# The second layer's first product made of seven block products over pairs of 384 tokens, its weights split ahead of time and read back

## The chip, the cores and the metric

The kernel runs on one core of a Trainium2 chip. The metric is the device time of one execution in microseconds (us), taken as the median of the runs shown. Work is spread over TensorE (PE in the profile: matmuls, with its weight loads as PEld), VectorE (DVE), ScalarE (ACT), GpSimd (POOL) and the DMA queue that SyncE (SP) issues.

## The reference

Attention over 4 batches of 8 heads gives x of 2304 tokens by 512, and two feed-forward layers follow. All of it is in float32.

```python
xn = x / np.sqrt(np.mean(x * x, axis=-1, keepdims=True) + 1e-06) * rms_g
g, val = xn @ w_gate, xn @ w_val              # layer one, 512 to 1536
y = (g / (1 + np.exp(-g)) * val) @ w_out      # 1536 to 512
h = y @ w_in                                  # layer two, 512 to 2048: its first product
r = np.maximum(h, 0.0)
out = (r * r) @ w_out2                        # 2048 to 512: its second product
```

## The kernel before

Activations lie with features on the partitions and tokens along the row. **A float32 product is three matmuls.** Each operand is kept as a high part, rounded to the type that TensorE multiplies, and a low part, the rest; `mm3` (L1177 to L1182) adds high times high, high times low and low times high into one PSUM bank, so a product of 128 outputs with a contraction of 512 is 4 x 3 = 12 matmuls. The matmul lines L1180, L1181 and L1182 are these three, for every product of both layers.

The tokens go in five blocks (`BLOCKS`: four of 512 and one of 256). Each layer is cut into two phases over its hidden features (`PHASES`): layer one into two of 6 hidden tiles, layer two (phases 2 and 3) into two of 8 tiles of 128. In a phase all blocks run past the same weights, and for each block and hidden tile j, `ff_in` makes the hidden tile (in layer two 12 matmuls into a `gv` bank), `after_in` finishes it (layer two: ACT takes the relu out of PSUM at L1272, DVE multiplies it with the PSUM value at L1276, and the high part, L1283 or L1285, and the low part, L1290, are made), and `ff_out` (12 matmuls into the four `a` banks) adds it to the block's output one tile later. A block's first half of the sum goes out to `yp_d` and comes back for the second phase's eviction (L1384). Layer one's result goes to `y_d` and is read and split again for each of layer two's phases (`load_task`, `split_tasks`, L870 and L885).

**Weights** come packed in two words each. `w_task` loads two matrices (1 MB, `wst<-in_w`), puts the words together in five DVE or ACT steps of 1024 columns (L1106 or L1108, L1115, L1118, L1124, L1129) and splits them into high (L1138 or L1140) and low parts (L1146) in a ring of 13 places.

**Order.** A planner written in the kernel runs while the program is built. Every step is a task with a due number and a cost on an engine; `advance` takes the step that can start first, and among those within `TOL` of it the one with the lowest due number. What it settles is the fixed order of each engine's queue. PE's own order is written out by hand at the end (`steps`): `ff_in` of a tile, then `ff_out` of the tile before.

Of the kernel before, what the change touches and what calls it, by code (L numbers as in the profile page):

```python
# [49 lines left out]
NMAX = 512  # L50
# [42 lines left out]
PHASES = [(1, 0, 6, True, False), (1, 6, 6, False, True), (2, 0, 8, True, False), (2, 8, 8, False, True)]  # L93
# [90 lines left out]
def kernel(ctx: ExitStack, tc: tile.TileContext, loc, strd, w1, w2, g, cst, out):  # L184
    nc = tc.nc

    def pool(name, bufs, stack=ctx, **kw):
# [7 lines left out]
    wr_p = pool("wr", RING)  # L195
    wst_p = pool("wst", WST)
    x_p = pool("xhl", 2)
    hid_p = pool("hid", 2)
    tmp_p = pool("tmp", 2)
    ys_p = pool("ys", 1)  # L200
# [15 lines left out]
    norm0 = const.tile([128, BLOCKS[0][1]], F32)  # L216
# [7 lines left out]
    y1_d = [dram.tile([128, KDM, n], F32, name=f"y1_d{i}") for i, (_, n) in enumerate(BLOCKS)]  # L224
    yp_d = {
        ly: [dram.tile([128, KDM, n], F32, name=f"yp{ly}_d{i}") for i, (_, n) in enumerate(BLOCKS)]
        for ly in (1, 2)
    }
    src_d = [None, xn_d, y1_d, y1_d]
# [50 lines left out]
    def advance():  # L280
# [32 lines left out]
        near = [f for f in found[e] if -100 < f[1] < min(-40, due - 3) and f[0] < start + half]  # L313
# [539 lines left out]
    def split_tasks(key, due, n, src, before=None, after=None, got=None):  # L853
# [4 lines left out]
        def hi(k):  # L858
            def f(_, t):
                if "t" not in cell:  # L860
                    cell["t"] = x_p.tile([128, 2, KDM, NMAX], F32R, tag="x", name="xt")
                    take("x")
                    turn("x")
                    xhl_of[key] = cell["t"]
# [133 lines left out]
    def load_task(ph, i, due):  # L998
# [3 lines left out]
        def load(_, t):  # L1002
            take("xs")
            cell["t"] = late["xs"].tile([128, KDM, NMAX], F32, tag="xs", name="xs")
            nc.sync.dma_start(out=cell["t"][:, :, :n], in_=src_d[ph][i])
            turn("xs")
            spawn(
                split_tasks((ph, i), due, n, lambda k: [(0, cell["t"][:, k, :n])], after=lambda t: give("xs", t)),
                lanes.dma(KDM * n, t),
            )  # L1010

        tasks.append(Task(due, [(
            lambda: "xs" in late and room("xs") and in_turn("xs", nth_x[ph, i] - NB) and ("src", ph, i) in done,
# [5 lines left out]
    def yp_task(ph, i, due):  # L1019
        n = BLOCKS[i][1]  # L1020
        nth = (NB if PHASES[ph][0] == 2 else 0) + i

        def load(_, t):
            take("yp")
            v = late["yp"].tile([128, KDM, NMAX], F32, tag="yp", name="ypt")
            nc.sync.dma_start(out=v[:, :, :n], in_=yp_d[PHASES[ph][0]][i])
# [6 lines left out]
            lambda: "yp" in late and room("yp") and in_turn("yp", nth) and ("yp", ly, i) in done,  # L1033
# [4 lines left out]
    wst, wt, wst_from, raws = {}, {}, {}, []  # L1038
    wst_free = [[WST, wst_p]]
    rings = [[RING, deque(), wr_p]]  # L1040
    mats = [
        (ph, j, m) for ph, (ly, _, nj, _, _) in enumerate(PHASES) for j in range(nj) for m in range(3 if ly == 1 else 2)
    ]
    loaded = iter(range(len(mats) // 2))
# [8 lines left out]
    def put_w(n, landed):  # L1053
        ph, j, m = mats[2 * n]
        ly, f0 = PHASES[ph][:2]
        wd = w1 if ly == 1 else w2
        src = next(r for r in wst_free if r[0])
        src[0] -= 1
        wst_from[n] = src
        t = src[1].tile([128, 2, 512, 2], I32, tag="wst", name="wst")  # L1060
        o = (f0 + j) * wd.shape[1] + m
        nc.sync.dma_start(out=t, in_=wd.rearrange("j m p c w -> p (j m) c w")[:, o:o + 2])
        wst[n] = t
        done["wst", n] = landed

    def ring_free():
        return [r for r in rings if len(r[1]) < r[0] or r[1][0]["t"] is not None]

    def ring_time():
        rs = ring_free()  # L1070
        r = next((r for r in rs if len(r[1]) < r[0]), rs[0])
        return 0.0 if len(r[1]) < r[0] else r[1][0]["t"]

    def ring_take():
        rs = ring_free()
        r = next((r for r in rs if len(r[1]) < r[0]), rs[0])
        if len(r[1]) == r[0]:
            r[1].popleft()
        cell = {"t": None, "n": 0}
        r[1].append(cell)  # L1080
        return r[2].tile([128, 2, 2, 512], F32R, tag="w", name="w"), cell
# [6 lines left out]
    def w_task(n, due):  # L1088
        cell = {}
        keys = mats[2 * n:2 * n + 2]  # L1090

# [6 lines left out]
        def size(parts, t):  # L1098
            cell["w"], cell["ring"] = ring_take()
            if "raw" in late:  # L1100
                cell["r"] = late["raw"].tile([128, 2, 512], F32, tag="raw", name="raw")
# [26 lines left out]
        def bits2(_, t):  # L1128
# [4 lines left out]
            wst_from.pop(n)[0] += 1  # L1133
            load_w(t)
# [7 lines left out]
        def lo(e):  # L1142
            def f(parts, t):
# [7 lines left out]
        before = mats[2 * (n - NRAW) + 1] if n >= NRAW else None  # L1151
        tasks.append(Task(due, [
            (
                lambda: in_turn("bits", n) and n in wst and bool(ring_free()) and (before is None or before in wt)
                and (keys[0][0] == 0 or "raw" in late),
                [dvx(1024, fast=True), [("A", 1.14)]], size,
                lambda: max(
                done["wst", n], ring_time(), done["w", before] if before else 0.0, done["late"] if keys[0][0] else 0.0
            ),
            ),  # L1160
# [3 lines left out]
            (None, [dvx(1024)], bits2, None),  # L1164
            (None, [act(1024), dvx(1024, fast=True)], hi, None),
# [3 lines left out]


# [429 lines left out]
```

## Time and profile before

| | |
|---|---|
| median of 3 runs | 929.5 us (927.97 to 931.24) |
| span of the profiled execution | 926.5 us |
| PE busy | 913.9 us, 99% |
| DVE busy | 584.0 us, 63% |
| ACT busy | 284.6 us, 31% |
| POOL busy | 41.8 us, 5% |
| layer two on PE | from 525.92 us to about 922.3 us |

The span runs from the first to the last instruction of one execution; the time of a run also holds what lies around it. Busy time counts an instruction from its start to its end, and two matmuls in a row overlap, so that the distance from start to start is shorter than the duration shown. The rows from which the argument is made stand in a section of their own below.

### The profile page before, as it was taken

Reading aid. Unit: us, or ns where it says so; the run is one execution under the profiler, and the core shown is the slowest. Engines: PE = TensorE matmul, PEld = TensorE weight load, DVE = VectorE, ACT = ScalarE, POOL = GpSimd, SP = SyncE. Lnnn points to the kernel's source line nnn. Section 1 sums busy time; section 2 is a strip of 40 time slices with the busy share of each in tenths; the row PEclk is TensorE's granted clock in tenths of the full one; section 3 lists DMA queues with packets and bytes.
Section 4 is the critical chain, followed back from the end, with each engine's and each line's share of the span. In section 5 each row is a group of like instructions: output and inputs, shape, how many; then the busy total and the mean of one; then the engine's idle time right before and its main releaser. Section 6 shows DMA issues by size and latency. Waiting matters only on the chain.

```text
span 926.5 us, 15562 instructions
## 1 busy us (share of the span) xinstructions
PE 913.9 (99%) x6466; PEld 766.0 (83%) x6466; DVE 584.0 (63%) x960; ACT 284.6 (31%) x773; POOL 41.8 (5%) x37
## 2 busy tenths in 40 slices
PE   8999999999999999999999999999999999999998
PEld 4778778888889888888888988888889888888888
DVE  6999956536879999352436999643438835344443
ACT  5987764322234332010102424121214211111110
POOL 0334400000000000000000000000000000000000
PEclk9999999999999999999999999999999999999999
DMA  9866742411725444130201545320203203030201
GB/s 331 268 230 200 238 148 75 136 48 65 277 92 182 160 137 159 68 110 5 91 24 62 179 146 181 137 90 24 91 1 137 69 1 136 1 114 1 69 10 59
DMA packets 38150, 105.41 MB, mean 114 GB/s; under 512 B 4160, under 2 KB 17472, under 8 KB 33984
## 3 DMA queue, kind: packets, MB, share of 16 engines
q1 hardware_dynamic: 38080, 104.41, 33.2%
q8 instruction: 51, 0.84, 0.4%
q14 instruction: 19, 0.16, 0.1%
HBM read 77.20 MB, written 23.59 MB: 109 GB/s over the span
## 4 chain that ended last, share of the span: by engine, by line
PE 94%; DVE 2%; DMA 2%; ACT 1%; issue 0%; SPq 0%; DVEq 0%; ACTq 0%
PE gv L1180 18%; PE gv L1181 18%; PE gv L1182 17%; PE a L1180 12%; PE a L1181 12%; PE a L1182 12%; DMA wst<-in_w 2%; PE xo L526 1%; PE sc L390 1%; ACT sm L438 1%; PE bc L832 0%; DVE raws L1118 0%; PE ms L574 0%; PE msb L810 0%; PE a L481 0%; DVE hd L1290 0%
## 5 line engine op out<-in xcount | busy, mean ns | idle before, releaser
L1180 PE MATMUL gv<-xt,w 128*128 128x512 f32 (+1 forms) x800 | 296.7, 371 | 0.5 <-DVE t L1260 0.5
L1181 PE MATMUL gv<-xt,w 128*128 128x512 f32 (+1 forms) x800 | 294.6, 368 | 0.0
L1182 PE MATMUL gv<-xt,w 128*128 128x512 f32 (+1 forms) x800 | 294.4, 368 | 0.0
L1180 PE MATMUL a<-hd,w 128*128 128x512 f32 (+1 forms) x560 | 207.4, 370 | 0.0
L1181 PE MATMUL a<-hd,w 128*128 128x512 f32 (+1 forms) x560 | 206.2, 368 | 0.1
L1182 PE MATMUL a<-hd,w 128*128 128x512 f32 (+1 forms) x560 | 206.1, 368 | 0.0
L1180 PEld LDWEIGHTS gv<-xt,w 128*128 128x128 f32 x800 | 150.8, 189 | 26.1 <-DVE t L1260 0.6
L1182 PEld LDWEIGHTS gv<-xt,w 128*128 128x128 f32 x800 | 150.8, 189 | 25.2
L1181 PEld LDWEIGHTS gv<-xt,w 128*128 128x128 f32 x800 | 150.9, 189 | 24.6 <-DVE xt L880 0.3
L1276 DVE TENSOR_TENSOR t<-t,gv 128x512 f32<-128x512 f32 (+1 forms) x80 | 50.6, 633 | 165.0 <-ACT t L1272 165.0
L1272 ACT ACTIVATE t<-gv 128x512 f32<-128x512 f32 (+1 forms) x80 | 44.4, 555 | 296.8 <-PE gv L1182 296.8
L1180 PEld LDWEIGHTS a<-hd,w 128*128 128x128 f32 x560 | 105.6, 188 | 18.2 <-ACT pt L493 0.3
L1182 PEld LDWEIGHTS a<-hd,w 128*128 128x128 f32 x560 | 105.6, 188 | 17.6
L1181 PEld LDWEIGHTS a<-hd,w 128*128 128x128 f32 x560 | 105.6, 189 | 17.4 <-DVE hd L1290 0.3
L1290 DVE TENSOR_TENSOR hd<-t,hd 128x512 fp32r<-128x512 f32 (+1 forms) x138 | 89.2, 646 | 4.6
L1260 DVE SCALAR_TENSOR_TENSOR t<-t,gv 128x512 f32<-128x512 f32 (+1 forms) x60 | 37.9, 631 | 84.3 <-ACT t L1256 84.2
L1256 ACT ACTIVATE t<-gv 128x512 f32<-128x512 f32 (+1 forms) x48 | 26.1, 545 | 191.4 <-PE gv L1182 191.2
L1268 DVE TENSOR_TENSOR t<-t,gv 128x512 f32<-128x512 f32 (+1 forms) x60 | 37.9, 632 | 40.6 <-PE gv L1182 40.2
L1285 DVE CAST hd<-t 128x512 fp32r<-128x512 f32 (+1 forms) x133 | 53.1, 399 | 9.3
L885 DVE TENSOR_TENSOR xt<-xs,xt 128x512 fp32r<-128x512 f32 (+1 forms) x56 | 33.0, 648 | 0.2 <-ACT xt L870 0.2
L1146 DVE TENSOR_TENSOR w<-raw,w 128x512 fp32r<-128x512 f32 x48 | 31.6, 686 | 0.7 <-ACT w L1138 0.5
L1124 DVE SCALAR_TENSOR_TENSOR raw<-wst,raw 128x1024 int32<-128x1024 int32 x25 | 30.6, 1223 | 0.6
(96 smaller groups left out, 676.7 us busy)
## 6 DMA issues: line engine op xcount, KB each, us to landing
wst<-in_w SPq DMA_DIRECT2D x34, 1024.0 KB, 5.8
yp_d<-ys SPq DMA_DIRECT2D x8, 1024.0 KB, 4.7
ypt<-yp_d SPq DMA_DIRECT2D x8, 1024.0 KB, 7.0
xs<-y_d SPq DMA_DIRECT2D x8, 1024.0 KB, 5.1
qk<-in_strd SPq DMA_DIRECT2D x8, 604.0 KB, 6.3
qk<-in_loc SPq DMA_DIRECT2D x8, 592.0 KB, 4.7
xs<-xn_d SPq DMA_DIRECT2D x4, 1024.0 KB, 4.8
y_d<-ys SPq DMA_DIRECT2D x4, 1024.0 KB, 4.8
```

The source lines that it names most:

```text
L885: eng.tensor_tensor(out=cell["t"][:, 1, k, c], in0=x, in1=x_hi, op=ALU.subtract)
L1124: nc.vector.scalar_tensor_tensor(out=bits(), in0=word(1), scalar=-0x40000000, in1=bits(), op0=ALU.bitwise_and, op1=ALU.bitwise_or)
L1146: eng.tensor_tensor(out=w[:, 1], in0=cell["r"][:, e], in1=w[:, 0].bitcast(F32), op=ALU.subtract)
L1180: nc.tensor.matmul(out=o, lhsT=whi, rhs=x_hi, start=first, stop=False)
L1181: nc.tensor.matmul(out=o, lhsT=whi, rhs=x_lo, start=False, stop=False)
L1182: nc.tensor.matmul(out=o, lhsT=wlo, rhs=x_hi, start=False, stop=last)
L1260: nc.vector.scalar_tensor_tensor(out=t_sb[:, :n], in0=t_sb[:, :n], scalar=1.0, in1=ps[:, :n], op0=ALU.add, op1=ALU.mult)
L1268: nc.vector.tensor_tensor(out=t_sb[:, :n], in0=t_sb[:, :n], in1=ps[:, :n], op=ALU.mult)
L1272: nc.scalar.activation(out=tile_t()[:, :n], in_=ps[:, :n], func=ACTF.Relu)
L1276: nc.vector.tensor_tensor(out=t_sb[:, :n], in0=t_sb[:, :n], in1=ps[:, :n], op=ALU.mult)
L1285: nc.vector.tensor_copy(hid[key][0][:, 0, :n], tmps[key][:, :n])
L1290: eng.tensor_tensor(out=hd[:, 1, :n], in0=t_sb[:, :n], in1=hd[:, 0, :n].bitcast(F32), op=ALU.subtract)
```

## The change

Layer one keeps its phases and its order on PE. Layer two is rewritten. It still has two phases, each over half of the hidden features, but inside a phase the tokens go in three pairs (q) of 2 x 384, and the hidden features in four groups (j) of 2 x 128.

**The first product.** For a pair and a group the product is a 2 by 2 block product: two hidden tiles by two halves of the contraction (256 each), times two halves of the contraction by two token halves. Eight block products were needed; `PRODUCTS` lists seven (Winograd's form), on seven weight blocks (three plain, four sums) and seven token blocks (three plain, four differences). Each is 2 x 3 = 6 matmuls of 384 columns (L1791). P1, P6, P7 and P4 are added one after the other into one bank, A, and the bank's value is wanted in between. So a copy of A is taken after P1 (`s1`) before P6 may be added to it, another after P6 (`u2`) before P7, and the sum A + `s5` after P7 before P4; P5 has a bank D (copied as `s5`, then P3 is added) and P2 a bank C. The copies (L1812 on ACT or L1814 on DVE) and the sums (L1821, DVE) give the four hidden tiles; the fourth is a relu of A (L1832, ACT). Then come the square (L1844 and L1845 on ACT, L1847 on DVE), the high part (L1873 or L1875) and the low part (L1880).

**The second product** is as before, in matmuls of 384 columns. The first token half (n = 0) is added up between the products, one group later; the second half (n = 1) follows in eight steps at the end of the pair.

**The token blocks** are read from `y1_d` in four transfers a pair. Four differences (L1640), seven high parts (L1647 or L1649) and seven low parts (L1654) of 768 columns are made for each of the six pairs.

**The weights** of layer two are no longer used from where they are split. For each phase and group, `pieces` makes the four sums (L1278), splits all into high and low parts in two small stages (L1292 or L1294, L1315), stores them to DRAM (`wi_d`, `wo_d`, L1306), and `load2_task` reads them back (L1340), 1.75 MB for a group of `w_in` and 1 MB of `w_out`. The first phase's are made during layer one, the second's mostly during the first two pairs.

All pools become fixed places in four large tiles (`ra`, `rb`, `fa`, `fb`, with `wst_a`). The diff, cut to its core:

```diff
-PHASES = [(1, 0, 6, True, False), (1, 6, 6, False, True), (2, 0, 8, True, False), (2, 8, 8, False, True)]
+PHASES = [(1, 0, 6, True, False), (1, 6, 6, False, True)]
+SN, NQ, NJ = 384, NT // 768, 4
+PRODUCTS = [
+    ("P1", 0, 0, "A", None), ("P5", 3, 1, "D", None), ("P6", 4, 2, "A", "s1"), ("P2", 1, 3, "C", None),
+    ("P7", 5, 4, "A", "u2"), ("P3", 6, 5, "D", "s5"), ("P4", 2, 6, "A", "c22"),
+]
...
+            o, w, x = c[role]["ap"][:, :SN], w_in(j), x_slot2(b)
+            for k in range(2):
+                w_hi, w_lo = (w[:, e, 256 * a + 128 * k:256 * a + 128 * k + 128] for e in range(2))
+                for n, (l, r) in enumerate(((w_hi, x[:, 0, k]), (w_hi, x[:, 1, k]), (w_lo, x[:, 0, k]))):
+                    nc.tensor.matmul(
+                        out=o, lhsT=l, rhs=r, start=need is None and k + n == 0, stop=k == 1 and n == 2,
+                        skip_group_check=need is not None,
+                    )
...
+            "P1": lambda: copy("s1", "A"), "P5": lambda: copy("s5", "D"), "P6": lambda: copy("u2", "A"),
+            "P2": lambda: add("s1", "C", 0, 0), "P7": lambda: add("s5", "A", 1, 1), "P3": lambda: add("u2", "D", 0, 1),
+            "P4": lambda: relu(1, 0),
...
+            steps = [
+                total(1024, 512, 768, ALU.add), total(1280, 1024, 0, ALU.subtract),
+                total(1536, 0, 512, ALU.subtract), total(1792, 256, 1280, ALU.subtract),
+            ]
...
+                nc.sync.dma_start(out=dst.bitcast(F32), in_=src)
...
-        for m in range(2 if PHASES[sl[0]][0] == 1 else 1):
+        for m in range(2):
             steps += ff_in(*sl, m)
...
+    for ph in (2, 3):
+        for q in range(NQ):
+            for j in range(NJ):
+                ps = [product(ph, q, j, p) for p in range(len(PRODUCTS))]
+                if j:
+                    a = [a_step(ph, q, 0, j - 1, h) for h in range(2)]
+                    row = ps[:3] + a[:1] + ps[3:6] + a[1:] + ps[6:] if j < NJ - 1 else ps[:4] + a[:1] + ps[4:] + a[1:]
+                elif ph == 2 and q == 0:
+                    row = ps[:3] + [last_out] + ps[3:]
+                else:
+                    row = ps
...
+            for n, js in ((0, [NJ - 1]), (1, range(NJ))):
+                for j in js:
+                    for h in range(2):
+                        steps += a_step(ph, q, n, j, h)
```

**Three places in the order of instructions.** First PE in layer two. Before, somewhere in the third phase: the last matmuls of a hidden tile into a `gv` bank and the first of the output step into the `a` banks.

```order
L1180 MATMUL gv_6371<-xt_5986,w_4165 128x512
L1181 MATMUL gv_6371<-xt_5986,w_4165 128x512
L1182 MATMUL gv_6371<-xt_5986,w_4165 128x512
L1180 MATMUL a0_6320<-hd_6368,w_4086 128x512
L1181 MATMUL a0_6320<-hd_6368,w_4086 128x512
L1182 MATMUL a0_6320<-hd_6368,w_4086 128x512
```

After, at the start of the first pair of the last phase: here bank A is `a0`, D is `pb0` and C is `a1`; the eighth row is P1 of the next group, in bank `pg1`, and the last is the first matmul of an output step.

```order
L1791 MATMUL a0_5419<-ra_72 128x384 x6
L1791 MATMUL pb0_5296<-ra_72 128x384 x6
L1791 MATMUL a0_5419<-ra_72 128x384 x6
L1791 MATMUL a1_5420<-ra_72 128x384 x6
L1791 MATMUL a0_5419<-ra_72 128x384 x6
L1791 MATMUL pb0_5296<-ra_72 128x384 x6
L1791 MATMUL a0_5419<-ra_72 128x384 x6
L1791 MATMUL pg1_5391<-ra_72 128x384 x6
L1791 MATMUL pb1_5306<-ra_72 128x384 x6
L1791 MATMUL pg1_5391<-ra_72 128x384 x6
L1354 MATMUL pg0_5340<-ra_72,rb_3119 128x384
```

In a group's first row of seven, P6, P7 and P4 (third, fifth, seventh) each go into a bank whose value another engine must have taken since, with one product of other banks between.

Second, DVE in the same places. Before, it does three things for a hidden tile:

```order
L1276 TENSOR_TENSOR t_7469<-t_7469,gv_7444 128x512
L1285 CAST hd_7472<-t_7469 128x512
L1290 TENSOR_TENSOR hd_7472<-t_7469,hd_7472 128x512
L1276 TENSOR_TENSOR t_7500<-t_7500,gv_7475 128x512
L1285 CAST hd_7503<-t_7500 128x512
L1290 TENSOR_TENSOR hd_7503<-t_7500,hd_7503 128x512
```

After, for the group whose matmuls stand above: the sums after P2, P7 and P3, and then the copy of the next group's A (`pg1`) after its P1.

```order
L1821 TENSOR_TENSOR fa_76<-a1_5420,fa_76 128x384
L1847 SCALAR_TENSOR_TENSOR fa_76<-fa_76 128x384
L1821 TENSOR_TENSOR fa_76<-a0_5419,fa_76 128x384
L1821 TENSOR_TENSOR fa_76<-pb0_5296,fa_76 128x384
L1880 TENSOR_TENSOR ra_72<-fa_76,ra_72 128x384
L1847 SCALAR_TENSOR_TENSOR fa_76<-fa_76 128x384
L1814 COPY wst_a_80<-pg1_5391 128x384
```

One queue now holds work that PE waits for within one product, and work that nobody waits for soon.

Third, DVE in layer one's second phase. Before, while its second block runs, only the four steps of a hidden tile stand in the queue:

```order
L1260 SCALAR_TENSOR_TENSOR t_4366<-t_4366,gv_4340 128x512
L1268 TENSOR_TENSOR t_4366<-t_4366,gv_4353 128x512
L1285 CAST hd_4382<-t_4366 128x512
L1290 TENSOR_TENSOR hd_4382<-t_4366,hd_4382 128x512
L1260 SCALAR_TENSOR_TENSOR t_4411<-t_4411,gv_4385 128x512
```

After, in the same block, steps of layer two's weights stand between them:

```order
L1435 SCALAR_TENSOR_TENSOR fa_76<-fa_76,gv_4190 128x512
L1443 TENSOR_TENSOR fa_76<-fa_76,gv_4209 128x512
L1452 CAST ra_72<-fa_76 128x512
L1457 TENSOR_TENSOR ra_72<-fa_76,ra_72 128x512
L1315 TENSOR_TENSOR wst_a_80<-fb_3115,wst_a_80 128x512
L1294 CAST wst_a_80<-fb_3115 128x256
L1315 TENSOR_TENSOR wst_a_80<-fb_3115,wst_a_80 128x256
L1158 TENSOR_SCALAR fb_3115<-wst_a_80 128x1024
L1165 TENSOR_SCALAR fb_3115<-fb_3115 128x1024
L1168 TENSOR_SCALAR fb_3115<-fb_3115 128x1024
L1174 SCALAR_TENSOR_TENSOR fb_3115<-wst_a_80,fb_3115 128x1024
L1435 SCALAR_TENSOR_TENSOR fa_76<-fa_76,gv_4242 128x512
```

Work of the weights has moved ahead of layer two, in among the steps for which layer one's matmuls wait. Up to this phase the order on PE, DVE, ACT and POOL is the same in both kernels.

## Rows read from the trace of the kernel before

**Rows 1.** The page: engines' busy time (share) xinstructions; the chain that ended last.

```profile
PE 913.9 (99%) x6466; PEld 766.0 (83%) x6466; DVE 584.0 (63%) x960; ACT 284.6 (31%) x773; POOL 41.8 (5%) x37
PE 94%; DVE 2%; DMA 2%; ACT 1%; issue 0%; SPq 0%; DVEq 0%; ACTq 0%
```

**Rows 2.** Timeline of PE where layer two begins: start us, duration us, instruction.

```profile
525.92 0.40 PE L1180 MATMUL gv<-xt,w 128*128 128x512 f32 x1
...
528.67 0.28 PE L1180 MATMUL a<-hd,w 128*128 128x256 f32 x1
...
530.10 0.40 PE L1180 MATMUL gv<-xt,w 128*128 128x512 f32 x1
```

**Rows 3.** The same timeline where a block of 256 tokens runs.

```profile
705.84 0.28 PE L1180 MATMUL gv<-xt,w 128*128 128x256 f32 x1
705.96 0.28 PE L1181 MATMUL gv<-xt,w 128*128 128x256 f32 x1
...
708.72 0.28 PE L1180 MATMUL gv<-xt,w 128*128 128x256 f32 x1
```

**Rows 4.** Timeline of all engines at the end (weight loads left out).

```profile
918.78 0.28 PE L1182 MATMUL gv<-xt,w 128*128 128x256 f32 x1
...
919.10 0.38 ACT L1272 ACTIVATE t<-gv 128x256 f32<-128x256 f32 x1 [2.50 <-PE gv L1182]
...
919.51 0.42 DVE L1276 TENSOR_TENSOR t<-t,gv 128x256 f32<-128x256 f32 x1 [1.60 <-ACT t L1272]
...
920.22 0.28 PE L1182 MATMUL a<-hd,w 128*128 128x256 f32 x1
920.37 0.42 DVE L1290 TENSOR_TENSOR hd<-t,hd 128x256 fp32r<-128x256 f32 x1
920.39 0.39 PE L1180 MATMUL a<-hd,w 128*128 128x256 f32 x1
920.85 0.39 PE L1181 MATMUL a<-hd,w 128*128 128x256 f32 x1
...
922.15 0.28 PE L1182 MATMUL a<-hd,w 128*128 128x256 f32 x1
```

**Rows 5.** Groups by shape: xcount | busy us, mean ns of one | idle before, releaser.

```profile
L885 DVE TENSOR_TENSOR xt<-xr,xt 128x384 fp32r<-128x384 f32 x4 | 2.2, 550 | 0.0
L1272 ACT ACTIVATE t<-gv 128x512 f32<-128x512 f32 x64 | 38.3, 598 | 264.0 <-PE gv L1182 264.0
L1272 ACT ACTIVATE t<-gv 128x256 f32<-128x256 f32 x16 | 6.1, 384 | 32.8 <-PE gv L1182 32.8
L459 DVE TENSOR_TENSOR sm<-sm,ri 128x768 f32<-128x768 f32 x5 | 4.7, 947 | 0.1
L1276 DVE TENSOR_TENSOR t<-t,gv 128x512 f32<-128x512 f32 x64 | 43.9, 686 | 152.1 <-ACT t L1272 152.1
L1276 DVE TENSOR_TENSOR t<-t,gv 128x256 f32<-128x256 f32 x16 | 6.7, 419 | 12.9 <-ACT t L1272 12.9
L1124 DVE SCALAR_TENSOR_TENSOR raw<-wst,raw 128x1024 int32<-128x1024 int32 x25 | 30.6, 1223 | 0.6
L1118 DVE TENSOR_SCALAR raw<-raw 128x1024 int32<-128x1024 int32 x25 | 17.2, 689 | 0.4
L1285 DVE CAST hd<-t 128x512 fp32r<-128x512 f32 x105 | 44.8, 427 | 7.4
```

**Rows 6.** Stretches: us, busy of PE, PEld, DVE, ACT, POOL (x), clock, DMA share, GB/s.

```profile
305.00:345.00 40.00, 40.00 (x183) 33.35 (x183) 36.45 (x55) 12.86 (x16) 0.00 (x0) 1.00 0.41 139
345.00:530.00 185.00, 185.00 (x918) 157.44 (x918) 104.39 (x171) 33.28 (x55) 2.84 (x2) 1.00 0.26 90
526.00:600.00 74.00, 74.00 (x334) 61.44 (x333) 64.60 (x97) 22.28 (x33) 1.56 (x1) 1.00 0.47 163
```

**Rows 7.** DMA issues: form xcount, KB each, median us from issue to landing.

```profile
wst<-in_w SPq DMA_DIRECT2D x34, 1024.0 KB, 5.8
out<-ys SPq DMA_DIRECT2D x4, 128.0 KB, 1.8
```

## What I expect, and why

> **What bounds the kernel now.** I read the page's busy times first, then the chain of work that ended last. PE is busy for 99% of the span and holds 94% of the chain [rows 1]: the end moves with PE's work, and other engines count only where PE waits for them. In the stretches after the attention PE is busy for all of the time, even where DVE is busy for 36.45 of 40 us [rows 6]. So the question has two parts: how much PE time the seven products save, and how many waits come in their place.
>
> Next the timeline of PE gives the price of a matmul from start to start. Of 256 columns: 24 in 708.72 - 705.84 = 2.88 us, 0.120 us each [rows 3]. Layer two begins at 525.92 and its last matmul starts at 922.15 [rows 2, 4]; with one more step of 0.12 that is 396.35 us. From this go the 12 matmuls of layer one's last output step, which stand inside it (530.10 - 528.67 = 1.43 us, rows 2): **layer two takes 394.9 us of PE**. In it are 5 blocks x 16 tiles x 24 = 1920 matmuls: 384 of 256 columns (46.1 us), 1536 of 512. The only wait is at the end, for the last hidden tile: 920.85 - 920.22 against 2 x 0.12, plus a slow step behind it; the twelve took 922.27 - 920.34 = 1.93 us for 1.44, so 0.5 us [rows 4]. Left for 512 columns: (394.9 - 46.1 - 0.5) / 1536 = 0.2268 us. Both prices are the columns at 2.4 GHz plus 0.013 us, so **384 columns should cost halfway, 0.1734 us**.
>
> [...]
>
> **The change part by part.** *Matmuls.* Per pair and group there are now 7 x 6 = 42 in the first product and 48 in the second, all of 384 columns. With 3 pairs, 4 groups, 2 phases that is 24 x 90 = 2160, at 0.1734 us 374.5 us. Saved: 394.9 - 374.5 = **20.4 us**. The columns alone (an eighth of the first product) would give 23.0 us; the 240 additional matmuls take back 3. No matmul of 384 columns with a weight load of its own stands in these traces as a stream, but one of 256 does, and there the load is hidden; so I take no extra.
>
> *Hand-overs in a bank.* This is the term the trace does not show. Count from a group's P1; a product takes 6 x 0.1734 = 1.04 us. How long the way through another engine is: from the start of a tile's last matmul to ACT 919.10 - 918.78 = 0.32 us, 0.20 after its step; ACT to DVE next to nothing; DVE's end (920.37 + 0.42) to PE 0.06 [rows 4]. A DVE step of 384 columns takes 0.55 us; ACT out of PSUM lies between 0.384 and 0.598, some 0.49 [rows 5].
> P6 is due at 2.08 and needs `s1`: 1.04 + 0.20 + 0.55 + 0.06 = 1.85. P7 in a group with no output step between (the first of a pair) is due at 4.16 and needs `u2`: 3.12 + 0.20 + 0.49 + 0.06 = 3.87. P4 there is due at 6.24 and needs the sum after P7: 5.20 + 0.20 + 0.55 + 0.06 = 6.01. In a pair's last group P7, P3 and P4 follow each other too. That makes 24 + 6 + 12 = 42 tight hand-overs, each with 0.23 to 0.29 us to spare if the engine is free when the bank is. All others have 2.08 us of output step between.
> Is it free? In the DVE order at the start of a pair: sum after P2 4.36 to 4.91, square to 5.46, sum after P7 to 6.01 (PE may go at 6.07, due 6.24), sum after P3 6.48 to 7.03, low part and square to 8.13; the next P1 ends at 8.32, its copy can start at 8.52. So there it holds, by 0.2 us. In the pair's last group a difference and a low part of 768 columns (0.947 each) stand ahead of the same sum; laid out likewise, DVE is through about when P7 is. And in the first group of all, evictions of layer one and a weight step of 0.69 stand between the sums and the copy, which then starts some 0.5 us late. Bounds: 0, if all fit; 42 x 0.25 = 10.5 if each is met by half a step in the way. A gain is excluded, as nothing here runs before its data. I take **1.5 us**, six late ones, near the lower end, since the places laid out mostly fit.
>
> [...]
>
> *DVE and ACT as a whole.* By the order, DVE has 396 steps behind the start of layer two; by shape at the durations of rows 5 these are 240 us against some 376 of PE. In the first pair, which also makes the second phase's weights, from its first sum to the next pair's 54 us in 62.4 (360 matmuls); in a later one 36. It carries them.
>
> *Layer one's second phase.* From 345 to 530 us DVE was busy for 104.39 of 185 us [rows 6]. Its queue for that part now holds 131 steps for layer two: 22 of 1024 columns at 1.223, 30 at 0.689, 26 of 512 at 0.686, 26 of 256 at 0.419, 17 casts at up to 0.427, 10 of 768 at 0.947, together some 93 us [rows 5], beside 85 us of layer one's own, counted the same way. So about 177 of 185: dense. But in 305 to 345 DVE was as dense (91%) and PE lost nothing [rows 6]; layer one's steps have output matmuls between them as cover. If that cover fails here, a step of 1.22 us in front of a hidden tile's high and low part costs up to 1 us, a handful of times: bounds 0 and 5. I take **0.5 us**.
>
> *Reading back.* A 1 MB transfer lands in 5.8 us [rows 7], so by bytes a group's 1.75 MB takes about 10. The first phase's first two groups are read before layer two starts. The last must wait on SP for layer one's last output step and is used by the fourth group, 1.4 + 7.3 + 2 x 11.4 = 31.5 us after layer two's start (42 matmuls in the first group, 66 in the next two); that output step is through at 3 x 1.04 + 1.43 = 4.6 us, so there are 27 us of cover for 10. Behind it on SP wait y1's last block (wanted by the third pair) and the second pair's tokens, wanted 30 us later. In the second phase a place is free when the last pair is through with its group, a pair less a group ahead, some 50 us. Cost nothing; if this cover were gone, 10 us a group.
>
> *The end.* The last steps' hidden tiles are split earlier, so the old 0.5 us wait (counted in 394.9) goes. The last eviction is 0.13 us longer (0.55 for 0.419) and the last stores hold 192 KB for 128, which landed in 1.8 us: **0.3 us** more.
>
> Sum: 926.5 - 20.4 + 1.5 + 0.5 + 0.3 = 908.4 us of span. The median of the runs shown lies 929.5 - 926.5 = 3.0 above that span: **911.4 us**, 0.981 of before.
>
> **The rivals.** *All fits.* Neither hand-overs nor layer one cost anything: 926.5 - 20.4 + 0.3 + 3.0 = 909.4. It falls within the forecast's case.
> *DVE is late again and again.* For it: the dense queue before layer two and 54 of 62 us in the first pair, where steps of 1.22 us that cannot be broken off stand in front of sums; and 0.2 us to spare is less than any step. Against it: from the third pair on the weights are done. With 10.5 us of hand-overs and 5 in layer one the time is 926.5 - 20.4 + 15.5 + 0.3 + 3.0 = 924.9; half of it, 917.
> *No change, because the saving does not show.* If the weight load were not hidden behind 384 columns and each matmul cost as one of 512, 2160 x 0.2268 = 489.9 us, 95 more; rows 3 speak against it. That case would be far slower; I give it 1 in 100.
> *Slower by the chain through one bank.* P1, copy, P6, copy, P7, sum, P4 is one chain in bank A. If DVE or ACT, which take their queue in order, were a whole 768-column step (0.947) away at each of the 42 tight places, each costs 0.947 - 0.25 = 0.70 us, 29 us in all, and the time is 926.5 - 20.4 + 29.3 + 0.5 + 0.3 + 3.0 = 939.2. It decides from (20.4 - 0.8) / 42 = 0.47 us of wait at each place on. Against it: such steps stand in the queues in the last groups and behind, not in all groups.
>
> **How the numbers follow.** About 0.3% (2.8 us) is what a measurement can tell from no change here. Forecast with up to 4 us of waits, 909 to 914: 0.64. Late again and again, 914 to 926: 0.24. Waits that eat the saving to within 0.3%, 927 to 932: 0.05. Slower by the chain, or dear matmuls: 0.05. Better than 909, if 384 columns cost less than the halfway price: 0.02. So faster 0.90, same 0.05, slower 0.05. The range of 8 in 10 goes from 908.5 up into the second case, to 921.
>
> **What would show it.** In the changed kernel's timeline, matmuls of L1791 should start 0.173 us apart and PE should need about 376 us from the first of them to the end. PE's idle time should lie in front of L1791 with DVE's L1814 or L1821 or ACT's L1812 as the releaser, in all 1 to 4 us; waits in front of layer one's output steps with DVE's low part as releaser would say that the weights come in the way. A DMA as releaser in layer two, or 0.2 us between matmuls of 384 columns, would make the prediction wrong.

## The result, and the profile after

The changed kernel takes **919.3 us** (median of 4 runs, 917.09 to 921.43) against 929.65 us: a ratio of 0.989 (0.987 to 0.991). The forecast was 911.4 us with a range of 908.5 to 921. The sign and the range held, the size did not: of 18.1 us forecast, 10.4 came. The time fell into the second case, "DVE is late again and again".

The page of after, beside [rows 1]: busy times, then the chain that ended last.

```profile
PE 896.2 (98%) x6701; PEld 805.4 (88%) x6706; DVE 652.0 (71%) x1074; ACT 356.3 (39%) x924; POOL 70.7 (8%) x56
PE 91%; DVE 5%; DMA 2%; ACT 1%; issue 1%; SPq 0%; DVEq 0%; ACTq 0%
```

PE's busy time fell by 17.7 us, yet the span only from 926.5 to 915.3. DVE's share of the chain rose from 2% to 5%: PE now waits for it. Where layer two begins, beside [rows 2] (timeline of PE: start us, duration us, instruction, count):

```profile
525.39 3.29 PE L1791 MATMUL pb<-ra 128*128 128x384 f32 x18
528.51 0.28 PE L1354 MATMUL a<-ra 128*128 128x256 f32 x1
...
529.94 1.21 PE L1791 MATMUL pg<-ra 128*128 128x384 f32 x6
```

18 matmuls of 384 columns take 528.51 - 525.39 = 3.12 us, 0.1733 each: the halfway price of the forecast, 0.1734, to 0.0001. At the end, beside [rows 4]:

```profile
911.41 0.34 PE L1356 MATMUL a<-ra,rb 128*128 128x384 f32 x1
911.78 0.56 DVE L1947 TENSOR_TENSOR fa<-a,fb 128x384 f32<-128x384 f32 x1
```

So layer two lasts 911.41 + 0.17 - 525.39 - 1.43 = 384.8 us on PE. 2160 matmuls at 0.1733 are 374.4. **10.4 us are waits**, where the forecast had 1.5. The groups by shape name where (xcount | busy us, mean ns | idle in front, releasers):

```profile
L1791 PE MATMUL a<-ra 128*128 128x384 f32 x438 | 84.6, 337 | 4.9 <-DVE fb L1821 1.9 <-DVE wst_a L1821 0.9 <-DVE fa L1821 0.7
L1791 PE MATMUL pg<-ra 128*128 128x384 f32 x258 | 51.5, 336 | 1.7 <-DVE wst_a L1821 0.9 <-DVE fa L1821 0.8
```

Nearly all stand in front of the first product, released by a sum (L1821). The idle time shown is less than what is lost: a matmul of 384 columns is shown 0.34 us long where the next one starts 0.17 us after it, and the second matmul behind a wait starts 0.28 us after the first, not 0.17. So I took the distances from start to start of all 2160 matmuls. 13 places are late, by 9.9 us together; the rest is spread thinly over the others:

| where | places | lost, us |
|---|---|---|
| P4 in a pair's last group, five of six pairs | 5 | 6.0 |
| P6, P7, P4 in the first group and P6 in the third of the second pair | 4 | 2.9 |
| P6 elsewhere, 0.19 to 0.37 each | 4 | 1.0 |

The third line looks like the tight hand-over that I had counted, but only its two places in the first pair (0.5 us) are; the other two go in run 6 below, with the second line. The first two lines I had not seen. The timeline of the third pair's last group shows the first (weight loads and output matmuls left out):

```profile
693.92 0.56 DVE L1649 CAST ra<-fb 128x768 fp32r<-128x768 f32 x1
693.97 2.22 POOL L1640 TENSOR_TENSOR fb<-fb 128x768 f32<-128x768 f32 x1 [50.58 <-DVE fb L1640]
...
694.35 2.24 PE L1791 MATMUL a<-ra 128*128 128x384 f32 x12
694.40 2.01 DVE L1875 CAST ra<-wst_a 128x384 fp32r<-128x384 f32 x1
696.44 0.56 DVE L1880 TENSOR_TENSOR ra<-wst_a,ra 128x384 fp32r<-128x384 f32 x1
696.92 1.02 DVE L1821 TENSOR_TENSOR wst_a<-a,wst_a 128x384 f32<-128x384 f32 x2
...
697.52 1.31 PE L1791 MATMUL a<-ra 128*128 128x384 f32 x6 [0.93 <-DVE wst_a L1821]
```

P7 and P3 are the twelve matmuls at 694.35. P7 is through at 695.39, and its sum could start at 695.6. It starts at 696.92, because the cast ahead of it took 2.01 us, and P4 waits. The same cast takes 0.36 us where no GpSimd step runs beside it. It starts while POOL makes a difference of the next pair's token blocks, and ends 0.22 us after POOL does (693.97 + 2.22 = 696.19; 694.40 + 2.01 = 696.41). At four of the five places it is such a cast; in the first pair it is a low part of 768 columns, which took 2.60 us for 0.95. Of the 27 casts of L1875, the seven that start while POOL runs take 0.97 to 2.03 us, the other 20 at most 0.36.

The second is at the start of the second pair:

```profile
590.89 2.25 PE L1791 MATMUL a<-ra 128*128 128x384 f32 x12
...
593.18 0.49 ACT L1812 ACTIVATE fa<-a 128x384 f32<-128x384 f32 x1 [2.05 <-PE a L1791]
593.72 4.65 PE L1791 MATMUL a<-ra 128*128 128x384 f32 x24 [0.58 <-ACT fa L1812]
...
598.47 0.56 DVE L1821 TENSOR_TENSOR fa<-a,fa 128x384 f32<-128x384 f32 x1 [1.14 <-PE a L1791]
...
599.09 2.38 PE L1791 MATMUL a<-ra 128*128 128x384 f32 x12 [0.72 <-DVE fa L1821]
```

The twelve matmuls are P1 and P5. The copy of A that P6 needs could start 0.2 us after P1, at 592.1; ACT had been idle for 2 us. It starts 0.21 us after P5 (590.89 + 2.08 = 592.97). Likewise the sum after P7 starts 0.27 us after P3. Here bank A and bank D are two banks of one PSUM tile: the order lists P1, P5 and P6 as one row on tile `a0`, while at the place of the last phase that the section on the change shows, A is `a0` and D is `pb0`. Of the 24 groups, this holds for the first and third group of the second pair alone, and these are the places of the table's second line. Two places of the third line are its after-effects: in the second pair's second group (0.37 us) ScalarE's relu of the last A had waited for VectorE's sum out of the neighbouring bank and pushed the copy back, and at the start of the last phase (0.19 us) an eviction of the last pair's output waited for P1 in the neighbouring bank and stood ahead of the copy:

```profile
722.79 0.49 ACT L1949 ACTIVATE fa<-a 128x384 f32<-128x384 f32 x1 [2.11 <-PE a L1791]
723.18 0.48 ACT L1812 ACTIVATE fa<-a 128x384 f32<-128x384 f32 x1
```

### The profile page after: what moved, and what is told of

Same layout as the page of the kernel before. It is cut to its first block, busy times and chain, and to the rows that moved or that the text cites. A ratio compares the mean times of both kernels' runs of the same rounds, so it can differ in the third digit from the quotient of the medians.

```text
span 915.3 us, 16478 instructions
## 1 busy us (share of the span) xinstructions
PE 896.2 (98%) x6701; PEld 805.4 (88%) x6706; DVE 652.0 (71%) x1074; ACT 356.3 (39%) x924; POOL 70.7 (8%) x56
## 4 chain that ended last, share of the span: by engine, by line
PE 91%; DVE 5%; DMA 2%; ACT 1%; issue 1%; SPq 0%; DVEq 0%; ACTq 0%
PE gv L1354 11%; PE gv L1355 11%; PE gv L1356 11%; PE a L1354 9%; PE a L1356 9%; PE a L1355 9%; PE a L1791 8%; PE pb L1791 6%; PE pg L1791 5%; DMA wst_a<-in_w 2%; PE pb L1355 2%; PE pb L1356 2%; PE pb L1354 2%; PE pg L1355 2%; PE pg L1354 2%; PE pg L1356 2%
## 5 line engine op out<-in xcount | busy, mean ns | idle before, releaser
L1354 PE MATMUL gv<-ra 128*128 128x512 f32 (+1 forms) x360 | 134.8, 375 | 0.4 <-DVE fa L1435 0.4
L1355 PE MATMUL gv<-ra 128*128 128x512 f32 (+1 forms) x360 | 132.7, 369 | 0.0
L1356 PE MATMUL gv<-ra 128*128 128x512 f32 (+1 forms) x360 | 132.6, 368 | 0.0
L1791 PE MATMUL a<-ra 128*128 128x384 f32 x438 | 84.6, 337 | 4.9 <-DVE fb L1821 1.9
L1791 PEld LDWEIGHTS a<-ra 128*128 128x128 f32 x438 | 76.2, 188 | 7.6 <-DVE fb L1821 2.6
L1355 PE MATMUL a<-ra,rb 128*128 128x384 f32 (+2 forms) x232 | 78.8, 340 | 0.0
L1354 PE MATMUL a<-ra,rb 128*128 128x384 f32 (+2 forms) x232 | 78.8, 340 | 0.0
L1356 PE MATMUL a<-ra,rb 128*128 128x384 f32 (+2 forms) x232 | 78.8, 340 | 0.0
L1354 PEld LDWEIGHTS gv<-ra 128*128 128x128 f32 x360 | 67.9, 189 | 12.1 <-DVE fa L1435 0.6
L1356 PEld LDWEIGHTS gv<-ra 128*128 128x128 f32 x360 | 67.9, 189 | 11.4
L1355 PEld LDWEIGHTS gv<-ra 128*128 128x128 f32 x360 | 67.9, 189 | 11.0 <-DVE ra L922 0.3
L1354 PE MATMUL a<-ra 128*128 128x512 f32 (+1 forms) x200 | 74.8, 374 | 0.0
L1356 PE MATMUL a<-ra 128*128 128x512 f32 (+1 forms) x200 | 73.7, 368 | 0.0
L1355 PE MATMUL a<-ra 128*128 128x512 f32 (+1 forms) x200 | 73.7, 368 | 0.0
L1791 PE MATMUL pb<-ra 128*128 128x384 f32 x312 | 60.3, 334 | 0.0
L1791 PEld LDWEIGHTS pb<-ra 128*128 128x128 f32 x312 | 54.5, 188 | 0.1
L1791 PE MATMUL pg<-ra 128*128 128x384 f32 x258 | 51.5, 336 | 1.7 <-DVE wst_a L1821 0.9
L1791 PEld LDWEIGHTS pg<-ra 128*128 128x128 f32 x258 | 45.0, 188 | 3.0 <-DVE wst_a L1821 1.2
```

The costliest lines, as they stand in the source:

```text
L1354: nc.tensor.matmul(out=o, lhsT=whi, rhs=x_hi, start=first, stop=False)
L1355: nc.tensor.matmul(out=o, lhsT=whi, rhs=x_lo, start=False, stop=False)
L1356: nc.tensor.matmul(out=o, lhsT=wlo, rhs=x_hi, start=False, stop=last)
L1791: nc.tensor.matmul(out=o, lhsT=l, rhs=r, start=need is None and k + n == 0, stop=k == 1 and n == 2, skip_group_check=need is not None,)
```

## The experiments

The stretch before layer two moves by up to 5 us between runs of one kernel (525.4 us in the profile above, with a granted clock of 1.000 over the span; 530.0 in that of run 8, with 0.994). So beside times I give the **length of layer two**, from the start of the first matmul of L1791 to the start of the last matmul of all: 386.0 us in the changed kernel. Lines of the later kernels stand up to three lower, in runs 9 and 10 up to five. In runs 3 and 6 the steps on VectorE, ScalarE and GpSimd keep their order; in 2, 4, 5 and 7 the planner lays VectorE's and ScalarE's queues out anew, so that more changes there than the steps that are moved.

**1. POOL's steps left out.** VectorE's, ScalarE's and the DMA queue's orders stay the same to the row.

```diff
-                eng = nc.gpsimd if parts[0][0] == "P" else nc.vector
-                eng.tensor_tensor(out=src, in0=xs_part(*add[0]), ...
+                if parts[0][0] != "P":
+                    nc.vector.tensor_tensor(out=src, in0=xs_part(*add[0]), ...
...
```

The low parts (L1654) have the same edit.

> The eleven steps of the token blocks that GpSimd makes in the changed kernel (eight differences, three low parts) are left out; the order on VectorE, ScalarE and the DMA queue is the same to the instruction. In the changed kernel five of six pairs lose 1.08 to 1.27 us in front of P4 of the last group (5.97 us of 9.95 us that layer two loses), each time behind a VectorE cast that took 2.0 us instead of 0.36 (once a low part that took 2.60 instead of 0.95) while GpSimd made a difference. Theory A (the cast is held because GpSimd reads at the same time): the cast takes 0.36 us, all five waits go, the span falls by 6.0 us from 915.3 to 909.3. Rival B (VectorE's queue is too dense at the end of a pair, the long cast only fills a wait for something else): the sum is late all the same, less than 2 us are gained.

Layer two fell to 380.9 us, the time to 915.2 us, 0.983 of before (0.981 to 0.985). All five waits in front of the last group's P4 went. The casts of L1875 (ns: min/median/max; first the changed kernel, then this one):

```profile
L1875 DVE CAST ra<-wst_a x8: 351/360/2033, 694.4 to 903.5; 128x384 fp32r<-128x384 f32 x8
```

```profile
L1875 DVE CAST ra<-wst_a x8: 352/354/361, 696.2 to 901.9; 128x384 fp32r<-128x384 f32 x8
```

Theory A holds: the same queue in the same order, without POOL beside it, has no long cast and no late P4. The gain is 5.1 us, not 6.0: P6 in the first pair's last group now loses 0.9 us, where it lost 0.25 (and 0.6 in run 8, the same kernel), and P4 in the last phase's first group 0.3, where it lost nothing.

**2. All token blocks on VectorE.**

```diff
-                (lambda: sums_done() is not None, [dvx(n), gps(n)], total, sums_done)
+                (lambda: sums_done() is not None, [dvx(n)], total, sums_done)
...
-                (None, [dvx(n), gps(n)], lo, None),
+                (None, [dvx(n)], lo, None),
```

> The token blocks of layer two are kept off GpSimd: VectorE makes all differences and low parts. The same eleven steps then cost VectorE 11 x 0.947 = 10.4 us, and the planner lays out its queue anew. Theory A (held casts): the five waits in front of P4 go, the span is 909 to 911. Rival B (density): two further steps of 0.95 us stand in the last group of each pair, and P4 waits as before or longer: 914 us or more.

385.0 us, and 917.2 us in all, 0.987 (0.985 to 0.989), with a span of 914.4 on B's side. But the five waits went here too, and something else came. Timeline of PE, then the stretches behind (us; busy of PE, PEld, DVE, ACT, POOL; granted clock; DMA share, GB/s):

```profile
536.28 1.14 PE L1791 MATMUL pb<-ra 128*128 128x384 f32 x5 [2.74 <-DVE ra L1654]
537.25 4.85 PE L1791 MATMUL pg<-ra 128*128 128x384 f32 x18
541.95 0.33 PE L1354 MATMUL a<-ra,rb 128*128 128x384 f32 x1
```

```profile
537.70:541.00 3.30, 3.30 (x12) 3.30 (x11) 2.83 (x3) 1.69 (x5) 0.00 (x0) 0.50 1.04 377
541.00:545.00 4.00, 4.00 (x24) 4.00 (x24) 2.15 (x4) 0.97 (x2) 0.00 (x0) 0.99 1.06 397
```

In the first group of all, P4 needs the last token block, whose low part POOL had made in the changed kernel. In VectorE's queue it stands behind the group's sums and layer one's evictions, and P4 goes on 2.9 us late; behind that wait the granted clock stands at 0.50 for 3 us, and 18 matmuls of 384 columns take 541.95 - 537.25 = 4.70 us from start to start instead of 18 x 0.1733 = 3.12, another 1.6. So B is right for the first pair and A for the others.

**3. Banks of a group in different tiles.** `bank_take` gets the tiles that the group holds, and takes a bank from another if there is one.

```diff
-        b = min((b for b in banks if bank_time(b) is not None), key=bank_time)
+        b = min(..., key=lambda b: (b["tile"] in beside, bank_time(b)))
...
```

> Only the choice of PSUM bank changes: the banks A, D and C of a group are taken from different tiles where that can be had. In the changed kernel A and D lie in one tile in two groups of 24, both in the second pair, and there P6, P7 and P4 lose 2.94 us in all; the copy after P1 starts 0.21 us after the end of P5, not of P1. Theory C (the wait is set by tile, so the copy waits for the next product): these waits fall to 0.3 us or less each, the span falls by 2.5 to 3 us from 915.3 to about 912.6; the five waits behind the held casts stay. Rival D (VectorE and ScalarE are late there because of the second phase's weights): no change within 1 us.

The waits of the second pair's first group went (P6, P7 and P4 lose nothing there), but layer two is 387.5 us long and the time 918.6 us, 0.988 (0.986 to 0.991): no gain. Now A of one group and A of the next often share a tile, and in seven groups P6 loses 0.40 to 0.74 us; six of them had lost 0.37 us or nothing. In six of the seven, A lies in the tile of the A before it, and there is no other group of which this holds. The first of them in the last phase:

```profile
734.63 0.49 ACT L1832 ACTIVATE wst_a<-a 128x384 f32<-128x384 f32 x1 [1.38 <-PE a L1791]
...
735.16 0.56 DVE L1814 COPY wst_a<-a 128x384 f32<-128x384 f32 x1 [1.07 <-ACT wst_a L1832]
...
735.77 1.31 PE L1791 MATMUL a<-ra 128*128 128x384 f32 x6
```

The copy of the new A waits for ScalarE's relu of the old A, another bank of the tile. That is theory C at work in another place, so my edit was wrong, not the theory.

**4. Both edits.**

> Token blocks off GpSimd and the banks of a group in different tiles. If A and C hold and nothing else takes their place, 5.97 + 2.94 = 8.9 us go: span 906.4, time about 908.2 (the changed kernel's time lay 1.8 us above its span). What stays is the tight hand-overs that the prediction counted, some 1 us in four places. If density is what limits, 912 or more.

921.2 us, 0.990 (0.987 to 0.992), layer two 385.9 us, so nothing of the 8.9 us that were expected to go: the new losses of 2 and of 3 came together, the late low part (3.0 us) and the copies (0.4 to 0.7 us a place). The next two runs have either edit in a better form.

**5. VectorE for the blocks, except the first pair's.**

```diff
-                (lambda: sums_done() is not None, [dvx(n), gps(n)], total, sums_done)
+                (..., [dvx(n)] if nth else [dvx(n), gps(n)], total, sums_done)
...
```

> GpSimd keeps its one step of the first pair's token blocks (with it on VectorE, P4 of the first group waited 2.74 us for that low part and the clock fell to 0.50 for 3 us behind it), and VectorE makes all blocks of the later pairs. Measured from the first matmul of L1791 to the start of the last matmul, since the stretch before it moves by up to 5 us from run to run: 386.0 us in the changed kernel. Theory A (held casts alone): 386.0 - 6.0 = 380.0. Rival B (density of VectorE): 384 or more.

382.2 us, between A's 380.0 and B's 384, and 916.6 us in all, 0.986 (0.984 to 0.988). The P4 waits fell from 6.0 to 0.75 us in all, 0.53 of it in the first pair. Part of the gain was lost again where A and D share a tile (P4 there 1.46 us for 0.99), in front of an output step of the second pair (0.5 us) and in the first pair.

**6. Tiles of their own for the products.** Products take `pb` and `pg`, each a tile of one bank, where these are free; the sums of the first token half take the paired tiles.

```diff
+            key=lambda b: (b["tile"] in beside, (b["tile"][0] == "a") != paired, bank_time(b)),
...
-                    acc2[key] = [bank_take() for _ in range(KDM)]
+                    acc2[key] = [bank_take(paired=n == 0) for _ in range(KDM)]
```

> Only the choice of bank: A, D and C always come from different tiles, the next group's A from another tile than this group's, and the paired tiles go to the output sums of the first half. The blocks stay on GpSimd where the planner puts them. Theory C (waits by tile): the three waits of the second pair (2.94 us) go and none of the new ones of the last try (copies that waited for ScalarE's relu on the neighbouring bank) comes: 386.0 - 2.9 = 383.1 us from the first matmul of L1791 to the start of the last. The five waits of about 1.2 us in front of P4 stay. Rival D: no change within 1 us.

383.3 us against 383.1 expected, 917.0 us, 0.986 (0.984 to 0.988). The start of the second pair:

```profile
593.40 1.20 PE L1794 MATMUL a<-ra 128*128 128x384 f32 x6
594.44 1.20 PE L1794 MATMUL pb<-ra 128*128 128x384 f32 x6
594.64 0.49 ACT L1815 ACTIVATE fa<-a 128x384 f32<-128x384 f32 x1 [1.01 <-PE a L1794]
595.48 1.20 PE L1794 MATMUL a<-ra 128*128 128x384 f32 x6
```

The copy now starts 0.20 us after P1, and P6 1.04 after P5: C holds. All waits of the second pair's groups are gone except that of the last group's P4, and the five P4 waits stay at 1.1 to 1.2 us each. The two after-effects (0.6 us) are gone with them, which was not expected. That the total came so close is in part luck: 3.6 us went, and 1.0 came back (P6 in the first pair's last group loses 0.9 us for 0.26, P4 in the last phase's first group 0.3).

**7. Both, in the better form.**

> Both: blocks on VectorE from the second pair on, and banks in tiles of their own. 386.0 - 6.0 - 2.9 = 377.1 us from the first matmul of L1791 to the start of the last, of which 374.4 + 1.4 are matmuls; some 1.3 us of tight hand-overs stay. Against the changed kernel on the same chip 8 to 9 us less, 0.97 to 0.975 of before. If density limits, the gain is less than 6.

377.9 us against 377.1 expected. The time is **910.4 us, 0.979 of before (0.977 to 0.981)**, faster than both kernels, though not the 0.97 to 0.975 that was expected. All that is left of the waits, 2.0 us, lies in the first pair. The list of PE's waits has two (releaser: us, times, longest):

```profile
PE pg L1794 <- DVE fa L1817: 0.9, 1, 0.9
PE pg L1794 <- DVE fa L1824: 0.3, 1, 0.3
```

In front of the first stand a cast, a low part and a cast of the weights (0.41 to 0.69 us each) in VectorE's queue. The second is again a held step, this time behind a weight's low part on POOL (a low part of 0.95 us takes 2.05):

```profile
567.08 1.59 POOL L1315 TENSOR_TENSOR wst_a<-fb,wst_a 128x512 fp32r<-128x512 f32 x1 [7.80 <-ACT wst_a L1292]
...
567.44 2.05 DVE L1654 TENSOR_TENSOR ra<-fb,ra 128x768 fp32r<-128x768 f32 x1
```

**8. The changed kernel beside these three.**

> The changed kernel itself beside the three others, as their base: 0.989 of before by the first measurement, and 386.0 us from the first matmul of L1791 to the start of the last, whatever the clock does ahead of it.

919.9 us, 0.989 (0.987 to 0.991), layer two 386.4 us. Kernel 7 lies 9.5 us below it, 8.5 of them in layer two.

**9 and 10. The price of a tight hand-over.** On kernel 7, the sum after P7 made twice, then the copy after P1.

```diff
                 if role == "A":
+                    nc.vector.tensor_tensor(out=e["ap"](), in0=c[role]["ap"][:, :SN], in1=e["ap"](), op=ALU.add)
```

> Base is the kernel with blocks on VectorE from the second pair and banks in tiles of their own: 377.94 us from the first matmul of the first product to the start of the last, 2.0 us of waits. Here the sum after P7 is made twice, one behind the other, in every group (so the values are not the reference's); nothing else moves. Its trace shows the second of two such steps 0.47 us behind the first, and 0.22 us to spare in front of P4 in the first and last group of a pair, 2.3 us and more in the middle ones. Theory E (as the prediction counted: only a hand-over with one product between is tight): 12 places late by 0.47 - 0.22 = 0.25 us, with 0.11 us for the restart 0.36 each, 4.3 us, and none in the other 12: 382.2 us. Theory F (every hand-over costs once VectorE has more to do): 24 x 0.36 = 8.6 us, 386.6.

383.5 us, so 5.5 us for 4.3 expected, and the waits stand where E had them: P4 loses about 0.5 us more in the first and last group of each pair, nothing in any middle group. The first group of the third pair:

```profile
664.42 1.20 PE L1794 MATMUL pb<-ra 128*128 128x384 f32 x6
...
664.72 0.55 DVE L1824 TENSOR_TENSOR fb<-a,fb 128x384 f32<-128x384 f32 x1
...
665.30 0.56 DVE L1826 TENSOR_TENSOR fb<-a,fb 128x384 f32<-128x384 f32 x1
...
665.92 0.97 PE L1794 MATMUL a<-ra 128*128 128x384 f32 x4 [0.29 <-DVE fb L1826]
```

The second sum starts 0.58 us behind the first, not 0.47, which is most of what the forecast lacked. With one sum PE could go on at 664.72 + 0.55 + 0.06 = 665.33, and P4 is due at 664.42 + 1.04 = 665.46: 0.13 us to spare.

```diff
+                    for _ in range(2 if what == "s1" else 1):
```

> Same base, 377.94 us. The copy after P1 is made twice in every group (the values stay the same); nothing else moves. P6 follows P1 with one product between in all 24 groups. Where VectorE copies (16 groups), 0.47 us more against 0.22 to spare: 0.25 + 0.11 us for the restart; where ScalarE does (8), 0.38 us more against 0.29: 0.09 + 0.11. Theory E: 16 x 0.36 + 8 x 0.20 = 7.4 us, 385.3 us. Rival G (P6 does not wait for this copy, or its slack is larger than counted): under 2 us.

387.6 us, 9.7 us for 7.4 expected. P6 is late in all 24 groups, by 0.34 us behind ScalarE's seven copies and 0.47 behind nearly all of VectorE's 17. Here too the second copy comes later than expected, 0.59 us behind the first on VectorE and 0.52 on ScalarE. Less the 0.11 us of the restart, that leaves 0.23 and 0.29 us to spare. The slack counted in the prediction is real and about as small as it said, and most hand-overs fit into it.

## Why the prediction was right and wrong

**The saving of 20.4 us: right.** 0.1733 us a matmul, 374.4 us for 374.5. The 2.4 GHz and the 0.013 us behind the halfway price are my estimate, a line through the two prices of before: 256 columns more cost 0.2268 - 0.1200 = 0.1068 us, 2.4 columns a ns, and 0.1200 - 0.1068 leaves 0.013. No trace shows a clock in GHz.

**The 42 tight hand-overs, as I had counted them: right.** (41, strictly: in the very first group layer one's last output step lies in front of P7.) Two of these places are late for no other cause than the queue, by 0.5 us in all, where I took six and 1.5. Runs 9 and 10 show 0.13 to 0.29 us to spare, and run 9 that a middle group's P4 is covered by the output step.

**The hand-overs' sum as a whole: wrong, by two things that are not in it.** Waits of 9.9 us for 1.5, and all but 0.5 of them at eleven of the same places: eight lose 0.85 to 1.27 us each, more than the 0.70 of the rival "slower by the chain". Only their small number kept the time in the range, and in that there is luck. First, I took every DVE step at its median duration and called a place fitting where these fit ("laid out likewise, DVE is through about when P7 is", for the last group). A cast of 0.36 us beside POOL took 2.0. That step failed: 6.0 us; run 1 shows the cause. The trace of before held the row that would have told me:

```profile
527.34 2.99 DVE L885 TENSOR_TENSOR xt<-xs,xt 128x512 fp32r<-128x512 f32 x3
528.23 1.56 POOL L1146 TENSOR_TENSOR w<-raw,w 128x512 fp32r<-128x512 f32 x1 [170.53 <-ACT w L1138]
```

Three low parts took 2.99 us, the last of them, begun beside a POOL step, 1.79 (the longest of L885), where [rows 5] had 0.686 for a step of 512 columns. I read that stretch for PE alone, and priced the move of blocks to POOL at nothing. In the changed kernel's layer two ten DVE steps take over 1.2 times the median of their line and shape, and all ten start while POOL runs: the seven casts of L1875, the low part of 2.60 us, and two sums of weights (L1278, 0.78 and 0.94 us for 0.42). Each ends 0.2 to 0.8 us after POOL's step. Sums that read PSUM take their 0.55 us beside POOL too (five in layer two). Why POOL holds the ones and not the others, no run shows.

Second, I counted banks as if each stood alone. The wait that the program sets is by tile, so a copy out of A waited for the product in D: 2.9 us in two groups, and 0.6 behind them; run 6 shows the cause. The names in the order (one tile for A and D) could have been read before.

**DVE's density: right in result, too high in size.** I had 177 of 185 us busy. The stretch after, beside [rows 6]:

```profile
345.00:530.00 185.00, 185.00 (x924) 158.20 (x923) 153.91 (x252) 38.92 (x66) 5.45 (x5) 1.00 0.67 239
```

154 us, and PE lost nothing: it is busy for all of the 185 us. Layer two begins at 525.39, 0.5 us earlier than before, where I had added 0.5; but that start moves by more from run to run. The durations of VectorE's steps in this stretch add up to 163.6 us: neighbours overlap by 10 us, which a sum of durations cannot see.

**Reading back: right.** No DMA releases PE in layer two. The loads of the second matrix (KB each, median us to landing) take a third longer than the 5.8 us that [rows 7] have for 1 MB, far inside the cover of 27 us:

```profile
rb<-wo_d SPq DMA_DIRECT2D x8, 1024.0 KB, 7.7
```

**The end: sign wrong, small.** From the last matmul's step to the span's end 915.3 - 911.58 = 3.7 us, before 926.5 - 922.27 = 4.2: 0.5 us less, where I had 0.3 more.

**Span and time.** 915.3 of span for 908.4: +8.8 in layer two, -1.0 at its start, -0.8 at the end. The median lies 4.0 us above the profiled span, where I had 3.0; the run itself had 917.09, so only 1.8 us lie around the span. The rest is scatter between runs, most of it in the stretch before layer two: in run 8's profile that stretch is 4.6 us longer, and layer two 0.4.

**The rivals.** "All fits" fell by the two causes above. "Late again and again" gave the size, but its reason, weight steps in front of sums, is worth 1 us or so (what is left in kernel 7's first pair is 2.0, of which 1.2 behind such steps and 0.5 behind POOL). "Dear matmuls" and "slower by the chain" fell with 0.1733 us and with waits in 13 places, not 42. With both causes taken away the kernel takes 910.4 us, 1.0 below the forecast; its layer two, counted as above, is 376.7 us for 376.0 in my sum, and the rest lies within the scatter.

## What to carry to other kernels

Before pricing a step that other engines wait for at its median, look for what runs on GpSimd beside it: in the changed kernel casts and a low part that started beside a GpSimd step ended 0.2 to 0.8 us after it (0.36 us became 2.0, and 0.95 became 2.6). Where a chain has tenths of a microsecond to spare, keep GpSimd away from that stretch, and give each bank of the chain a tile of its own. But move work off GpSimd only where VectorE has room: in the first pair the same edit cost a wait of 2.9 us (run 2), behind which the granted clock stood at 0.50 for 3 us.

## What the runs showed of the hardware that was not expected

- Each wait of PE at the 13 places of the table costs 0.11 us more than itself: the matmul behind the first one starts 0.28 us later instead of 0.17, at all of them.
- In run 2 PE idled for 2.74 us; of the matmuls behind it, 18 of 384 columns took 4.70 us, with a granted clock of 0.50 from 537.7 to 541.0. In run 4 a wait of the same 2.74 us was followed by 18 such matmuls in 3.12 us at a clock of 1.00. Why one and not the other is open.
- POOL's difference takes 1.85 us beside steps that read PSUM and 2.22 us at the four places where a cast of DVE had started 0.04 us ahead of it (693.92). There POOL's step is 0.37 us longer, and the next cast on DVE takes 2.0 us for 0.36.
